# Half sums of the second weights made earlier, and the last unit's block sums dealt otherwise, in a two-level Strassen-Winograd feed-forward stage

## The chip, the cores and the metric

The kernel runs on one core of one Trainium2 chip. The metric is device time in microseconds (us) of one execution. A core has five engines that run side by side, each in its own order: PE (TensorE, matrix products into the PSUM memory), DVE (VectorE), ACT (ScalarE), POOL (GpSimd) and SP (SyncE, which here only issues DMA transfers). They wait for one another through semaphores. In the profile PE stands for matrix products and PEld for the loading of the stationary operand, which runs beside them.

## The reference

Talking-heads attention (8 batches, 12 heads, 448 positions, 64 wide) makes x of 8 x 448 x 768. A Fourier mix and a feed-forward block follow; the change lies in the feed-forward block alone.

```python
X = np.fft.fft(x, axis=1)
X = np.fft.fft(X, axis=2)
mixed = np.real(X).astype(np.float32)
u = x + mixed
mu = np.mean(u, axis=-1, keepdims=True)
var = np.mean((u - mu) ** 2, axis=-1, keepdims=True)
un = (u - mu) / np.sqrt(var + 1e-06)
ch = np.maximum(un @ w_ch1, 0.0) @ w_ch2
return (u + ch).astype(np.float32)
```

`w_ch1` is 768 x 3072 and `w_ch2` 3072 x 768. Both arrive as 64-bit floats and are turned into 32-bit ones on the chip.

## The kernel before

**Tiling.** After the attention and the mix, the feed-forward block handles the 3584 rows in 7 blocks of 512 rows (index t) and the 3072 inner columns in 6 chunks (index c). One pass over a row block and a chunk is a *unit*, n = 7c + t, so there are 42 units. Each product of a unit is a Strassen-Winograd product of 2 x 2 blocks: seven block products instead of eight, with sums before and after. The blocks are `h11`, `h12` and so on of the activations h (after the ReLU), and blocks (r, d) of the result: r is the half of the rows, d the half of the columns.

**A unit.** `first(n, ...)` makes h from the normalized input `ub` and the weights `w1t`: seven products in the order `ORDER`, six pairs of matmuls each, so 42 places that are counted in `done`. Between them DVE and ACT bring the results out of PSUM into h (copies, sums, ReLU). In chunk 0, `second` multiplies h by the second weights directly. From chunk 1 on (`DEEP = 1`) `second2` does this at two levels: each of its seven products (in the order `ORDER2`) is again seven products of quarter blocks. For the inner level, `quarters` makes sums of the quarters of h (tile `hq`, four operations, on DVE or POOL), and `halves` makes sums of the quarters of the second weights (tile `wt`, and one in place in `w2t`; four operations of 128 x 192 each).

**Half sums.** The second weights change once a chunk, so `halves` runs only in the first unit of each deep chunk (t = 0): seven sets, called set 0 to set 6 below after their place in `ORDER2`. The code calls set k ahead of product k of `first`, on DVE when k is even and on POOL when k is odd (lines 1194 and 1195).

**Order of work.** In the deep part the order of PE, DVE, ACT and POOL is that of the program text; each of these engines works strictly in order. `second2` has a list `at` of what is to be done at which of its 64 steps; seven steps belong to one outer product j (b = 7j), and the inner products stand at steps b+0, b+3, b+4, b+5, b+8, b+13 and b+16. An inner product is called by `mm`; its result is copied from PSUM into a tile `od` by `take` (ACT, L1351) or added there by `more` (DVE, L1345). Inner products of one outer product share a PSUM tile, so the next inner product that adds to this tile waits until the last result was read: the matmul of step b+16 (`psP<-wt,h`) waits for `more` of step b+11. Steps 49 and later are woven into the next unit's `first` (table `SEAM` at its first ten places); step 0 is woven in two places before the end of its own `first`.

**Ahead of that step.** Near the end of `first` DVE does: L1226 (h22 plus the fifth product, which ACT then rectifies), two pieces of background work, L1231 (h21 plus the sixth product), L1251 and L1252 (sums hs1 and hs2), four operations of `quarters` for hs2, L1255 (h21 again), then `more` of step 11. POOL does `quarters` of h11 and h22 after the fifth product, and of h12 after the seventh. In seam units the calls of `halves` stand between these.

**Background work.** `wts.deal` gives out the conversion of the next chunk's weights in small pieces (DVE L256 to L308, POOL L252, ACT L263, DMAs by SP), so many per product as the table `DEALS` says. `load_w2` fetches the next chunk's second weights, one DMA for each outer product at step b+17 of the last unit of a chunk.

**Sums of the outer level.** `both` adds one `od` tile to another (128 x 768, L1354). `out_` sends an `od` tile to the output with an adding DMA, issued by POOL (L1357): it reads the block, adds and writes it back. Two adding DMAs to one block wait for each other. The last unit (`end`) does otherwise: at step 0 it loads the blocks 11, 12 and 22 of the output into tiles `v11`, `v12`, `v22`, adds to them in memory, and stores them with plain DMAs, one half of each by SP and one by ACT (`store`, L1361). Only block 21 goes out with an adding DMA. The results of its last outer product are added to `v12` directly. Two of the last unit's block sums are on POOL.

Of the kernel before, what the change touches and what calls it, by code (L numbers as in the profile page):

```python
# [1033 lines left out]
ORDER2 = (0, 3, 5, 6, 4, 1, 2)  # L1034
UB = {(0, 0): 0, (0, 1): 6, (1, 0): 1, (1, 1): 2}
TOTALS = ((4, 6, 0), (5, 2, 4), (6, 2, 6), (3, 1, 5))
DEEP = 1
DEALS = ((2, 2, 2, 2, 2, 0, 0), (3, 4, 4, 4, 3, 0, 0))
DEST = {0: (0, 0), 1: (0, 0), 4: (1, 1), 5: (0, 1), 2: (0, 1), 6: (1, 1), 3: (1, 0)}
ACC = {0: "P", 5: "P", 6: "P", 3: "P", 1: "Q", 4: "R", 2: "R"}  # L1040
# [3 lines left out]
def ffn_phase(ctx, tc, rest, ident, u_scr, u_rev, wts, ub_scr, out, fold_rest,  # L1044
# [4 lines left out]
    nc = tc.nc  # L1049
# [28 lines left out]
    def ps_tile(key):  # L1078

        n = taken[key] = taken[key] + 1  # L1080
        more = len(pps) > 3 and key != "Q" and n % 3 == 0
        return pps[3 if more else "QPR".index(key)].tile(
            [P, 512], F32, name="ps" + key, tag="ps" + key, bufs=1 if more else 2)

    def next_part():
        if parts:
            parts.pop(0)(lambda: ppx.tile([P, 512], F32, name="ms", tag="ms"))
# [25 lines left out]
    def new_ub(n, i):  # L1113
        ubs[n, i] = lead.ub_tile(pub)
# [4 lines left out]
    def stats(t, x):  # L1119
        if x == 0:  # L1120
            mvs[t] = pst.tile([P, NT2, 3], F32, name="mv", tag="mv", bufs=2)
        st = pst.tile([P, 2, 6], F32, name="st", tag="st")
        for y in range(2):
            nc.vector.bn_stats(st[:, y, :], us[t][x][:, y * DH:(y + 1) * DH])
        nc.vector.bn_aggr(mvs[t][:, x, 0:2], st[:, :, :])

    def power(t):
        lead.power(mvs[t])
# [31 lines left out]
    def quarters(eng, hq, h, f0, f1):  # L1160

        o = hq[:, f0:f1, :, :]
        a11, a12, a21, a22 = (h[:, f0:f1, f, x * P:(x + 1) * P]
                              for x in range(2) for f in range(2))
        for to, a, b, op in ((o[:, :, 0], a21, a22, ALU.add),
                             (o[:, :, 1], o[:, :, 0], a11, ALU.subtract),
                             (o[:, :, 2], a11, a21, ALU.subtract),
                             (o[:, :, 3], a12, o[:, :, 1], ALU.subtract)):
            eng.tensor_tensor(to, a, b, op=op)  # L1169

    def halves(i, eng):

        wt[i] = right["wt"].tile([P, 3, DQ], F32, name="wt", tag=f"wt{i}")
        b11, b12 = w2[i][:, 0, :DQ], w2[i][:, 0, DQ:]
        b21, b22 = w2[i][:, 1, :DQ], w2[i][:, 1, DQ:]
        t1, t2, t4 = (wt[i][:, x, :] for x in range(3))
        for to, a, b in ((t1, b12, b11), (t2, b22, t1), (b12, b22, b12), (t4, b21, t2)):
            eng.tensor_tensor(to, a, b, op=ALU.subtract)

    def first(n, st, beside):  # L1180

        c, t = divmod(n, NTB)
        deep = c >= DEEP
        seed = n >= NTB + 2
        h = st["h"] = ph.tile([P, 7, FM, HT], F32, name="h", tag="h")
        if deep:
            hq = st["hq"] = right["hq"].tile([P, 7, 4, P], F32, name="hq", tag="hq")
        h11, h22, h21, hs1, hs2, h12, h12s = (h[:, x] for x in range(7))
        norms = c == 0 and t + 1 < NTB
        vec = nc.vector  # L1190
        ps = {}
        done = 0
        for k, i in enumerate(ORDER):
            if deep and t == 0:
                halves(ORDER2[k], (nc.vector, nc.gpsimd)[k % 2])
            if i in OPENS and ACC[i] not in ps:
                ps[ACC[i]] = ps_tile(ACC[i])
            p = ps[ACC[i]].rearrange("p (m t) -> p m t", m=FM)
            ub = ubs.pop((n, i))
            for m in range(FM):  # L1200
                for kc in range(NK):
                    for fn in beside.pop(done, ()):
                        fn()
                    done += 1
                    mm = nc.tensor.matmul(p[:, m, :], w1[i][:, kc, m * P:(m + 1) * P],  # L1205
                                          ub[:, kc, :],
                                          start=i in (0, 4, 1)[:3 - seed] and m == kc == 0,
                                          stop=kc == NK - 1, skip_group_check=True)
                    if n == k == m == kc == 0:
                        tc.keep_in_program_order(mm)  # L1210
            if i == 0 and seed:
                ps["Q"] = ps_tile("Q")
                nc.scalar.copy(out=ps["Q"][:, :], in_=ps["P"][:, :])
            elif i == 0:
                nc.scalar.copy(out=h11, in_=p)
            elif i == 4:
                nc.scalar.copy(out=h22, in_=p)
            elif i == 5:
                nc.scalar.copy(out=h21, in_=p)  # L1219
            elif i == 1 and seed:  # L1220
                nc.scalar.activation(h11, p, ACTF.Relu)
            elif i == 1:
                vec.tensor_tensor(h11, h11, p, op=ALU.add)
                nc.scalar.activation(h11, h11, ACTF.Relu)
            elif i == 6:
                vec.tensor_tensor(h22, h22, p, op=ALU.add)  # L1226
                nc.scalar.activation(h22, h22, ACTF.Relu)  # L1227
                if deep:
                    quarters(nc.gpsimd, hq, h, H11, H22 + 1)
            elif i == 2:  # L1230
                vec.tensor_tensor(h21, h21, p, op=ALU.add)  # L1231
                nc.scalar.activation(h21, h21, ACTF.Relu)
            else:
                nc.scalar.activation(h12, p, ACTF.Relu)
            x = k - 2 * (n == 0)
            if norms and 0 <= x < NT2:
                stats(t + 1, x)
                if x == NT2 - 1:
                    power(t + 1)
            if (n == 0 and k < 2) or (n == 1 and k not in (1, 2)):  # L1240
                next_part()
                if n == 0 and k == 1:
                    fold_rest(8)
            if n == 0 and k == 5:
                fold_rest()
            if deep:
                wts.deal(DEALS[t > 0][k])
            elif i != 2:
                wts.deal(2 if norms else 3)
            if i == 2:  # L1250
                vec.tensor_tensor(hs1, h21, h22, op=ALU.add)  # L1251
                vec.tensor_tensor(hs2, hs1, h11, op=ALU.subtract)  # L1252
                if deep:
                    quarters(vec, hq, h, HS2, HS2 + 1)
                vec.tensor_tensor(h21, h11, h21, op=ALU.subtract)  # L1255
            if t == NTB - 1 and c + 1 < NC:
                load_w1(c + 1, i)
            if NTB <= n + 1 < NC * NTB:
                new_ub(n + 1, i)
                nc.sync.dma_start(out=ubs[n + 1, i][:, :, :],  # L1260
                                  in_=ub_scr[(n + 1) % NTB][i])
        if deep:
            quarters(nc.gpsimd, hq, h, H12, H12 + 1)
            wts.deal(0)
        else:
            vec.tensor_tensor(h12s, h12, hs2, op=ALU.subtract)
        assert not beside
# [34 lines left out]
    def second2(n, st):  # L1302
# [5 lines left out]
        vec = nc.vector  # L1308

        def on(s, fn, *a):  # L1310
            at.setdefault(s, []).append(lambda: fn(*a))
# [65 lines left out]
            if t == NTB - 1 and c + 1 < NC:  # L1377
                on(b + 17, load_w2, c + 1, i)
        j0, j3, j5, j6, j4, j1, j2 = range(7)
        v11, v12, v22 = range(7, 10)  # L1380
        pl = nc.gpsimd
        on(12, lambda: quarters(vec, st["hq"], st["h"], H21, H21 + 1))
        on(19, lambda: quarters(vec, st["hq"], st["h"], HS1, HS1 + 1))
# [1 line left out]
                                         st["h"][:, HS2], op=ALU.subtract))  # L1385
        on(20, lambda: quarters(pl, st["hq"], st["h"], H12S, H12S + 1))
        if end:
            for v, r, d in ((v11, 0, 0), (v12, 0, 1), (v22, 1, 1)):
                on(0, load, v, r, d)
            for s, *o in ((24, vec, v11, j0), (33, vec, j5, j0), (34, pl, v12, j5),  # L1390
                          (40, vec, j6, j5), (41, vec, j3, j6), (41, pl, v22, j6),
                          (47, vec, v22, j4), (48, vec, v12, j4), (54, vec, v11, j1)):
                on(s, both, *o)
            on(42, out_, j3, 1, 0)
            on(48, store, v22, 1, 1)
            on(55, store, v11, 0, 0)
            on(61, store, v12, 0, 1)
        else:
            for s, *o in ((33, j5, j0), (40, j6, j5), (47, j5, j4), (54, j0, j1),
                          (61, j5, j2), (62, j4, j6)):  # L1400
                on(s, both, vec, *o)
            on(27, out_, j3, 1, 0)
            on(44, out_, j6, 1, 0)
            on(55, out_, j0, 0, 0)
            on(62, out_, j5, 0, 1)
            on(63, out_, j4, 1, 1)
# [46 lines left out]
    with tc.manual_schedule(engines={ET.PE, ET.DVE, ET.Activation, ET.Pool}):  # L1453
        rest_ = {}
        for n in range(DEEP * NTB, NC * NTB):
            while parts_ and sum(o[1] for o in wts.ops) < 36:
# [82 lines left out]
```

## Time and profile before

| what | us |
|---|---|
| three runs | 2323.86, 2320.95, 2319.33 |
| their median | 2320.95 |
| the profiled execution | 2327.42 |
| its span | 2325.5 |

| engine | busy us | share of the span | instructions |
|---|---|---|---|
| PE | 2258.0 | 97% | 22894 |
| PEld | 1744.6 | 75% | 22894 |
| DVE | 1715.7 | 74% | 3629 |
| ACT | 1170.0 | 50% | 3336 |
| POOL | 1278.7 | 55% | 1783 |

A deep unit takes 34.2 us (PE's rows of the same product recur at this distance, 1316.96 to 1351.16 for example). The five units with half sums begin near 1110, 1347, 1589, 1832 and 2073 us; they are called *seams* here. The span is what lies between the first and the last instruction; the time of a run has some 2 us more. In the timeline, a row merges equal neighbouring instructions (x2, x12); its columns are start, duration, engine, line, operation, operands, and in brackets the idle time of the engine just before it with the instruction that ended it. A releaser is inferred: of several things waited for, the last one is named.

### The profile page before, as it was taken

The numbers are of one execution on the slowest core, as the hardware profiler recorded it, in microseconds if no ns is written. First come the engines' busy times: TensorE is split into PE (matmuls) and PEld (weight loads), VectorE is DVE, ScalarE is ACT, GpSimd is POOL, SyncE is SP. The second block draws the span as 40 slices with busy tenths as digits, with TensorE's granted clock in tenths as the row PEclk, the third lists the DMA queues.
The fourth block names the chain that finished last, engine by engine and source line by source line (L and its number), as shares of the span: only waits on it lengthen the run. The fifth ranks groups of instructions, "written<-read, shape, count | busy, mean of one in ns | idle before, by whom it ended". The sixth has DMA issues, their size and how long they took to land.

```text
span 2325.5 us, 60782 instructions
## 1 busy us (share of the span) xinstructions
PE 2258.0 (97%) x22894; PEld 1744.6 (75%) x22894; DVE 1715.7 (74%) x3629; ACT 1170.0 (50%) x3336; POOL 1278.7 (55%) x1783
## 2 busy tenths in 40 slices
PE   6999999999999999999999999999999999999998
PEld 2455555555555667676899999999999899999997
DVE  3778878888878747777777787878778777756545
ACT  4776767666676522221355445444445445434434
POOL 3587868878777532221555454555555545444333
PEclk9999999999999999999999999999999999999999
DMA  7575665656656366667777887878877977795663
GB/s 162 163 187 165 185 179 164 191 167 189 187 161 197 135 237 197 201 207 284 215 174 192 229 220 189 221 180 243 210 174 193 283 174 179 192 257 109 148 146 68
DMA packets 231920, 439.04 MB, mean 189 GB/s; under 512 B 39624, under 2 KB 154080, under 8 KB 231630
## 3 DMA queue, kind: packets, MB, share of 16 engines
q1 hardware_dynamic: 158318, 303.56, 38.2%
q0 software_dynamic: 67312, 129.64, 30.0%
q8 instruction: 183, 3.00, 0.6%
q10 hardware_dynamic: 6000, 1.97, 0.5%
q14 instruction: 107, 0.88, 0.1%
HBM read 213.16 MB, written 142.76 MB: 153 GB/s over the span
## 4 chain that ended last, share of the span: by engine, by line
PE 84%; DVE 4%; POOL 3%; DMA 3%; ACT 2%; issue 1%; SPq 1%; ACTq 0%; DVEq 0%; POOLq 0%
PE psP L1205 17%; PE psP L1323 13%; PE psR L1205 9%; PE psR L1323 6%; PE mx L652 6%; PE ms L716 5%; PE ms L624 5%; PE psQ L1205 4%; PE po L686 4%; PE psQ L1323 3%; PE psP L1282 3%; PE ms L841 2%; DMA Kr<-Sb 2%; PE psR L1282 2%; PE ms L598 1%
## 5 line engine op out<-in xcount | busy, mean ns | idle before, releaser
L1357 POOL DMA_DIRECT2D out_dram<-od x171 | 207.8, 1277 | 260.3 <-DVE od L1345 189.4
L676 POOL TENSOR_SCALAR PP<-PP,rcp 128x448 f32<-128x448 f32 x368 | 235.7, 650 | 195.2 <-DVE rcp L674 160.6
L666 ACT ACTIVATE PP<-mx,nmx 128x448 f32<-128x448 f32 x368 | 230.2, 631 | 168.6 <-DVE nmx L659 155.1
L659 DVE TENSOR_REDUCE nmx<-mx 128x1 f32<-128x448 f32 x368 | 212.6, 618 | 95.3 <-PE mx L652 92.0
L1169 POOL TENSOR_TENSOR hq<-h 128x128 f32<-128x128 f32 (+1 forms) x210 | 127.8, 609 | 262.7 <-ACT h L1227 127.4
L1351 ACT COPY od<-psP 128x192 f32<-128x192 f32 x488 | 156.1, 320 | 181.8 <-PE psP L1323 177.2
L1354 DVE TENSOR_TENSOR od<-od 128x768 f32<-128x768 f32 x211 | 201.8, 970 | 53.8 <-ACT od L1351 52.8
L487 ACT COPY Sb<-ms 124x448 f32<-124x448 f32 (+1 forms) x384 | 184.6, 540 | 55.8 <-PE ms L624 31.1
L624 PE MATMUL ms<-kT,qT 64*32 64x448 f32 (+1 forms) x3072 | 200.1, 548 | 12.8 <-ACT qT L487 6.3
L699 DVE STREAM_TRANSPOSE Pv<-po 128x896 f32<-128x896 f32 x184 | 203.7, 1107 | 6.1 <-PE po L686 5.7
L652 PE MATMUL mx<-Kr,kw 60*32 60x448 f32 x2944 | 194.7, 550 | 8.5 <-ACT PP L666 4.7
L716 PEld LDWEIGHTS ms<-Pv,vv 64*64 64x64 f32 x5376 | 138.1, 132 | 71.6 <-issue 48.1
L686 PE MATMUL po<-PP,kw 60*32 60x448 f32 x2944 | 187.3, 539 | 3.1 <-issue 1.9
L1205 PE MATMUL psP<-qs,w1t 128*128 128x256 f32 x744 | 179.1, 380 | 0.7 <-ACT h L1219 0.7
L1205 PE MATMUL psP<-ks,w1t 128*128 128x256 f32 x744 | 179.2, 380 | 0.1
L716 PE MATMUL ms<-Pv,vv 64*64 64x120 f32 (+1 forms) x5376 | 160.9, 263 | 1.5 <-ACT X L487 0.8
L252 POOL TENSOR_SCALAR wst<-wst 128x256 f32<-128x256 f32 (+1 forms) x76 | 119.2, 1576 | 68.4 <-ACT wst L263 67.0
L1205 PEld LDWEIGHTS psP<-qs,w1t 128*128 128x128 f32 x744 | 139.6, 190 | 17.3 <-ACT h L1219 1.1
L1205 PEld LDWEIGHTS psP<-ks,w1t 128*128 128x128 f32 x744 | 139.6, 190 | 16.5 <-DVE u L1287 0.7
L1323 PE MATMUL psP<-wt,h 128*128 128x192 f32 x490 | 120.5, 328 | 12.0 <-DVE od L1345 12.0
L1205 PE MATMUL psP<-ub,w1t 128*128 128x256 f32 x528 | 127.1, 379 | 0.0
L1226 DVE TENSOR_TENSOR h<-h,psP 128x512 f32<-128x512 f32 x42 | 28.8, 687 | 130.2 <-PE psP L1205 116.6
(190 smaller groups left out, 5303.5 us busy)
## 6 DMA issues: line engine op xcount, KB each, us to landing
Kr<-Sb SPq DMA_DIRECT2D x736, 105.0 KB
out_dram<-od POOLq DMA_DIRECT2D x171, 384.0 KB, 6.9
qs<-ub SPq DMA_DIRECT2D x89, 384.0 KB
ks<-ub SPq DMA_DIRECT2D x88, 384.0 KB
ub<-ub SPq DMA_DIRECT2D x79, 384.0 KB
w1t<-w SPq DMA_DIRECT2D x42, 384.0 KB
w2t<-w SPq DMA_DIRECT2D x42, 384.0 KB
raw<-in_moe_w_ch_dram SPq DMA_DIRECT2D x32, 384.0 KB
```

Of the source, the lines that this page charges most:

```text
L624: nc.tensor.matmul(pss[x][o:o + hi - lo, :S], st["qT", xx][64 * x:64 * x + 64, y, lo:hi], st["kT", xx][64 * x:64 * x + 64, y, :], start=Tr ...
L652: nc.tensor.matmul(mx[x][64 * z + o:64 * z + o + 32, :S], kw1[64 * x:64 * x + KR, o:o + 32], Kr[64 * x:64 * x + KR, z, :], start=True, sto ...
L659: nc.vector.tensor_reduce(nmx[:, :], steps[T]["mx"][x][:, :S], axis=AX.X, op=ALU.max, negate=True)
L666: nc.scalar.activation(steps[T]["PP"][:, x, :], steps[T]["mx"][x][:, :S], ACTF.Exp, bias=steps[T]["nmx", x][:, :], accum_out=steps[T]["den ...
L676: nc.gpsimd.tensor_scalar(PP[:, x, :], PP[:, x, :], rcp[:, x:x + 1], 1.0, op0=ALU.mult, op1=ALU.mult)
L686: nc.tensor.matmul(po[o:o + 32, z, :S], kw2[64 * z:64 * z + KR, y, :], PP[64 * z:64 * z + KR, :, c * HS:(c + 1) * HS], start=True, stop=True)
L699: nc.vector.transpose(turned[a]["Pv"][:, j, :].rearrange("p (z s) -> p z s", z=2), steps[T]["po"][:, :, :S])
L716: nc.tensor.matmul(pss[y][64 * x:64 * x + 64, :nu * R], st["v", pr][64 * y:64 * y + 64, x, jb * D:(jb + 1) * D], _ap(Pv, 64 * y * rp + 32 ...
L1205: mm = nc.tensor.matmul(p[:, m, :], w1[i][:, kc, m * P:(m + 1) * P], ub[:, kc, :], start=i in (0, 4, 1)[:3 - seed] and m == kc == 0, stop= ...
L1323: nc.tensor.matmul(ps[j, key][:, :DQ], a, b, start=m in (0, 4), stop=True, skip_group_check=True)
L1354: eng.tensor_tensor(D[j][:, :, :], D[j][:, :, :], D[k][:, :, :], op=ALU.add)
L1357: nc.gpsimd.dma_start(out=acc[t, r, d], in_=D[j][:, :, :], accum_op=ALU.add)
```

## The change

A table `HALVES` says at which product of `first` which set of half sums is made, and on which engine (0 is DVE, 1 is POOL). All sets keep their engine. Set 2 goes from product 2 to 1, set 3 from 3 to 2, set 4 from 4 to 3, set 5 from 5 to 4 and set 6 from 6 to 4. So all are called at the first five products; the background pieces of `DEALS` stay with their products.

In the last unit block 22 isn't loaded, summed in memory and stored any more. The tile of j4 (with j6 added to it on DVE) goes there with an adding DMA. Block 21 gets two adding DMAs, j3 at step 27 and j6 at step 41, instead of one of their sum at step 42. The sums j3 + j6 (DVE) and v22 + j6 (POOL) are gone, v22 + j4 becomes j4 + j6, and the remaining sums and stores stand up to three steps earlier.

```diff
+HALVES = {0: ((0, 0),), 1: ((1, 1), (2, 0)), 2: ((3, 1),), 3: ((4, 0),), 4: ((5, 1), (6, 0))}
...
             if deep and t == 0:
-                halves(ORDER2[k], (nc.vector, nc.gpsimd)[k % 2])
+                for j, eng in HALVES.get(k, ()):
+                    halves(ORDER2[j], (nc.vector, nc.gpsimd)[eng])
...
-        v11, v12, v22 = range(7, 10)
+        v11, v12 = 7, 8
...
         if end:
-            for v, r, d in ((v11, 0, 0), (v12, 0, 1), (v22, 1, 1)):
+            for v, r, d in ((v11, 0, 0), (v12, 0, 1)):
                 on(0, load, v, r, d)
+            on(27, out_, j3, 1, 0)
             for s, *o in ((24, vec, v11, j0), (33, vec, j5, j0), (34, pl, v12, j5),
-                          (40, vec, j6, j5), (41, vec, j3, j6), (41, pl, v22, j6),
-                          (47, vec, v22, j4), (48, vec, v12, j4), (54, vec, v11, j1)):
+                          (40, vec, j6, j5), (45, vec, v12, j4), (46, vec, j4, j6),
+                          (52, vec, v11, j1)):
                 on(s, both, *o)
-            on(42, out_, j3, 1, 0)
-            on(48, store, v22, 1, 1)
-            on(55, store, v11, 0, 0)
+            on(41, out_, j6, 1, 0)
+            on(47, out_, j4, 1, 1)
+            on(53, store, v11, 0, 0)
             on(61, store, v12, 0, 1)
```

## The prediction, made before the changed kernel was run

> **What bounds the kernel now.** I read the page first: PE is busy 97% of the span, its clock is full in all 40 slices, and it is 84% of the chain that ended last. So only what makes PE wait counts. In part 5 one deep group has PE idle before it:
>
> ```profile
> L1323 PE MATMUL psP<-wt,h 128*128 128x192 f32 x490 | 120.5, 328 | 12.0 <-DVE od L1345 12.0
> ```
>
> The waits of PE from 1085 us to the end agree (total, times, longest; the one other entry is 0.7 us):
>
> ```profile
> PE psP L1323 <- DVE od L1345: 12.4, 7, 2.5
> ```
>
> Seven waits. PE's timeline (start, us, in brackets the idle time before) finds five of them one chunk apart, one in the first unit of each deep chunk (a "seam"), and the longest of the last two at the end:
>
> ```profile
> 1131.05 0.59 PE L1323 MATMUL psP<-wt,h 128*128 128x192 f32 x2 [2.46 <-DVE od L1345]
> 1372.57 0.59 PE L1323 MATMUL psP<-wt,h 128*128 128x192 f32 x2 [1.81 <-DVE od L1345]
> 1614.25 0.59 PE L1323 MATMUL psP<-wt,h 128*128 128x192 f32 x2 [1.98 <-DVE od L1345]
> 1857.44 0.59 PE L1323 MATMUL psP<-wt,h 128*128 128x192 f32 x2 [1.81 <-DVE od L1345]
> 2098.95 0.59 PE L1323 MATMUL psP<-wt,h 128*128 128x192 f32 x2 [1.81 <-DVE od L1345]
> 2318.89 0.59 PE L1323 MATMUL psP<-wt,h 128*128 128x192 f32 x2 [2.08 <-DVE od L1345]
> ```
>
> The five seam waits sum to 9.87 us. DVE's timeline at the second seam shows why: set 6 of the half sums stands between the last sum of h and the addition (L1345) for which PE's step 16 waits.
>
> ```profile
> 1361.66 0.69 DVE L1226 TENSOR_TENSOR h<-h,psP 128x512 f32<-128x512 f32 x1 [1.09 <-POOL wt L1178]
> ...
> 1364.15 0.69 DVE L1231 TENSOR_TENSOR h<-h,psR 128x512 f32<-128x512 f32 x1 [1.14 <-PE psR L1205]
> ...
> 1370.32 0.60 DVE L1178 TENSOR_TENSOR wt<-w2t 128x192 f32<-128x192 f32 x1
> 1370.96 0.49 DVE L1178 TENSOR_TENSOR wt<-w2t,wt 128x192 f32<-128x192 f32 x1
> 1371.38 0.60 DVE L1178 TENSOR_TENSOR w2t<-w2t 128x192 f32<-128x192 f32 x1
> 1371.90 0.34 DVE L1178 TENSOR_TENSOR wt<-w2t,wt 128x192 f32<-128x192 f32 x1
> 1372.17 0.34 DVE L1345 TENSOR_TENSOR od<-od,psP 128x192 f32<-128x192 f32 x1
> ```
>
> The set takes 1.85 us here, PE loses 1.81: without it the addition has 0.04 us to spare. The brackets are DVE's room ahead of it.
>
> **What the Trainium skill says.** "SBUF — State Buffer", section "SBUF: two separate sides": a DVE operation with two SBUF inputs and a POOL operation share one pair of ports, "an exclusive lock, not a bandwidth split". The trace agrees: a half sum takes DVE 0.35 us alone and up to 0.74 beside POOL's half sums, POOL 0.58 to 0.70. "GPSIMD Engine Reference", section "3. Performance versus the Vector engine": two-input work is about 2x slower on POOL; here 0.58 against 0.35, 1.7x. "DMA: Bandwidth & Descriptors", section "Two DMAs through the same engine are not ordered": a DMA that depends on another waits for its semaphore at the issuing engine. The trace agrees: in a usual unit j6's adding DMA, ready at 2244.5, starts at 2246.29, 6.3 us after j3's on the same block.
>
> **The seams on DVE.** The order of instructions shows the change at all five: set 6 leaves its place after L1255 and stands before L1226, set 4 goes two background pieces earlier, set 2 before the last two block sums of the unit before. No DVE instruction is added there. The removed delay is 2.64, 1.85, 2.24, 1.85 and 1.85 us, the waits are 0.04 to 0.26 less, so all 9.87 goes if L1231 starts on time; it waits for PE's sixth product, and whatever it is late becomes PE's wait.
>
> Second seam, worked through: DVE was busy from 1344 to 1360.57 but for 0.27 us, then idle 1.09 and 1.14. Set 2 moves beside POOL's two DMA issues (1349.71 to 1352.14), 1.3 us for 2.27; set 4 beside the next two (from 1356.47), 1.4 for 2.46; set 6 takes 2.46. Net +2.46 - 0.97 - 1.06 - 0.27 = +0.2: ready at 1360.8, in time. Third: set 2 gains 0.6, set 4 0.9, set 6 costs 2.5; L1226 about 0.8 late, the 1.16 idle before L1231 absorbs it. Fourth: set 6 costs 2.4, set 4 gains 0.85, idle 0.93; L1226 about 0.65 late against 1.14. Fifth: idle 3.71 and 1.81, all absorbed. PE's seventh product reads L1226's tile only 2.3 us after L1226's usual start. Were set 6 fully contended (2.65) and nothing else gained, L1231 would be late by 0.15, 1.34 and 0.58 at seams 2 to 4, 2.1 in all: the upper bound on DVE. I take none, because POOL's DMA issues leave DVE its full pace in the trace.
>
> Does set 6 wait for its load? The last of the seven w2t loads leaves SP at 1349.9; the set is due at 1358.4. In the whole deep part one half sum waited for a load (1.6 us, at 1095). SP's other moves are weight loads and stores swapped with a neighbour, a chunk ahead of their use: nothing. The two block sums behind set 2 are up to 2 us later, and the DMAs that they release stand behind POOL's set 1 anyway (1356.47).
>
> **The seams on POOL.** Here the change has a price: set 5 now stands before the quarters of h11 and h22 instead of behind them. PE's step 3 needs their first result, step 4 the second. At seam 2 POOL had 0.48 us idle there; at the first seam none:
>
> ```profile
> 1122.45 0.58 POOL L1178 TENSOR_TENSOR wt<-w2t,wt 128x192 f32<-128x192 f32 x1
> 1123.01 0.72 POOL L1169 TENSOR_TENSOR hq<-h 128x256 f32<-128x256 f32 x1
> ```
>
> Set 5 took 2.71, 3.21, 3.04, 3.20 and 3.19 us. The second quarter follows 1.45 us after POOL is free (1.8 at seam 1). Seam 2: free at 1362.6, +3.2 +1.45 = 1367.25; PE's step 4 was at 1367.19, so I put 0.2. Seam 3: 1603.8 + 3.04 + 1.45 = 1608.3 against 1608.71. Seam 4: 1851.3 against 1852.06. Seam 5: 2091.3 against 2093.58. Seam 1: 1123.0 + 2.7 + 1.8, and 0.3 because set 3 now runs beside set 6, is 1127.8 against 1124.92: PE waits 2.6 to 2.9 there, where it waited 2.46; the late DVE is hidden behind it. I put -0.3; bounds +1.0 (an uncontended POOL, sets at 2.4) and -0.9.
>
> Seams: -0.3 + 1.6 + 1.98 + 1.81 + 1.81 = 6.9 us.
>
> **The last unit.** It loses a load and two stores, a sum on DVE and one on POOL. POOL's slow sum held DVE, and ACT's part of the store of block 22 held ACT (its copy at 2317.51 had stood 3.26 us):
>
> ```profile
> 2313.48 2.58 POOL L1354 TENSOR_TENSOR od<-od 128x768 f32<-128x768 f32 x1 [0.89 <-DVE od L1354]
> ...
> 2316.10 0.96 DVE L1354 TENSOR_TENSOR od<-od 128x768 f32<-128x768 f32 x1 [0.65 <-POOL od L1354]
> ```
>
> But from 2314.25 DVE has the same list as before: three block sums and seven short additions, and the sum of v11 now stands ahead of the addition that frees PE's last matmul; before, it ran beside it. At DVE's own durations: R at 2314.25, v12 to 2315.45, two additions to 2316.0, j4 to 2316.9, two more to 2317.45, v11 to 2318.35, addition to 2318.65, PE, last addition to 2320.05, where it was 2320.24: 0.2 gained at v12's store. The other candidate is block 22's adding DMA. POOL issues j3's after its quarters, at 2309.05; j6's waits for that landing, 6.3 us later at 2315.35; j4's follows at 2316.9 and lands in 6.4 to 8.3 us (adding DMAs from 2240 on), at 2323.3 to 2325.2. The closing drains of before stood at 2324.6. So the tail is between 0.8 gained and 1.5 lost; I take 0.1 gained.
>
> **Sum.** 6.9 + 0.1 = 7.0 us. The profiled execution took 2327.42 us (span 2325.5 and 1.9 around it): 2320.4 for its like. The shown runs' median, 2320.95, is 6.5 lower; they execute the same instructions, so I carry the 7.0 over: 2314.0 us, 0.30% less. A difference of 0.2%, 4.6 us, is about what a measurement of this kernel can tell from none.
>
> **The rivals.**
> A, the forecast: seams 2 to 5 cleared, seam 1 bound by POOL: 2314.0, own range 2312 to 2316. For it: the brackets above. Chance 0.58.
> B, sharing of the ports: set 6 wholly contended (2.1 lost), and POOL's set 5 slowed as its first operation was after a DMA issue (1.65 and 2.18 us at seams 2 and 3 for 0.6 to 1.0), 1.2 at each of the first two seams: 7.0 - 2.1 - 2.4 = 2.5, so 2318.5; with DVE's part alone 2316.1. For it: half sums on both engines at once. Against: no DMA issue stands just ahead of set 5. Chance 0.24.
> C, all five cleared and 0.8 at the end: 2320.95 - 10.7 = 2310.3. Needs POOL 2.5 us faster at seam 1. Chance 0.10.
> D, slower: POOL becomes the bound. If it comes x us later to step 4 than worked out, the stalls are x at seams 1 and 2, x - 0.4, x - 0.8 and x - 2.3 at the others. At x = 2.8 these sum to 10.5 and the change loses 3.5; at 4 they sum to 16.5 and it loses 9.5: 2330. It decides from about x = 2.1, where they reach 7.0. Against: POOL's paces are measured beside a busy DVE already, and the set that it would be late by is already counted. Chance 0.08.
> That the half sums aren't moved is excluded by the order of instructions.
>
> **How the numbers follow.** Over 0.2% faster is below 2316.3: all of A but a tenth, C, and a quarter of B: 0.52 + 0.10 + 0.06, and I say 0.70 as B's lower end lies near it. Slower is D, 0.08; the rest, 0.22, is no change. The range runs from C's 2310 to just past B's 2319.5 and leaves out D and a little at either end.
>
> **What would show it.** Right: the waits of PE for L1345 fall from 12.4 us to under 3; at seams 2 to 5 step 16 has no bracket; at seam 1 PE waits at psR or psP (wt,hq) for POOL's hq, 2 to 3 us. DVE's set 2 takes about 1.3 us at seam 2, and L1231 keeps its bracket there. At the end no POOL sum stands before DVE's. Wrong: brackets for hq at seams 2 to 4, L1231 starting late without one, or the drains waiting for block 22's DMA after v12's store has landed.

## The result, and the profile after

| | us, median | lowest to highest | runs |
|---|---|---|---|
| before | 2324.84 | 2318.81 to 2336.50 | 22 |
| after | 2317.72 | 2310.47 to 2321.05 | 22 |

The ratio is 0.9964, 95% interval 0.9955 to 0.9973: 0.36% faster. The changed kernel, run once more in another comparison, gave 0.9979 (0.9968 to 0.9990). The profiled execution took 2313.94 us, its span 2312.0, 13.5 less than before.

The waits of PE from 1085 us to the end, in the trace of after (total, times, longest):

```profile
PE psP L1325 <- DVE od L1347: 2.6, 2, 1.4
PE psP L1207 <- DVE h L1228: 1.9, 2, 1.1
PE psP L1325 <- POOL hq L1170: 0.7, 2, 0.5
PE psR L1325 <- ACT h L1236: 0.7, 1, 0.7
```

All lines after the new table have moved: L1226 is now L1228, L1231 is L1233, L1345 is L1347 and so on. The row that read 12.4 us in seven waits is down to 2.6 in two. PE's timeline says where the waits of after are:

```profile
1115.66 1.99 PE L1207 MATMUL psP<-qs,w1t 128*128 128x256 f32 x8 [0.79 <-DVE h L1228]
1119.52 0.59 PE L1325 MATMUL psR<-wt,hq 128*128 128x192 f32 x2 [0.67 <-ACT h L1236]
1120.64 0.59 PE L1325 MATMUL psP<-wt,hq 128*128 128x192 f32 x2 [0.54 <-POOL hq L1170]
1600.25 0.59 PE L1325 MATMUL psP<-wt,hq 128*128 128x192 f32 x2 [0.17 <-POOL hq L1170]
1837.94 1.99 PE L1207 MATMUL psP<-ub,w1t 128*128 128x256 f32 x8 [1.14 <-DVE h L1228]
2301.76 0.56 PE L1325 MATMUL psP<-w2t,hq 128*128 128x192 f32 x2 [1.21 <-DVE od L1347]
2304.39 1.01 PE L1325 MATMUL psP<-wt,h 128*128 128x192 f32 x2 [1.42 <-DVE od L1347]
```

The first three are at seam 1, then one each at seams 3 and 4, and two in the last unit; no step 16 at a seam has a bracket. (The 0.67 is POOL's too: its first quarter ended at 1119.46, 0.06 before the matmul; ACT's L1236 is merely the last releaser on record.) DVE's timeline at seam 2, to be held against the rows at 1361.66 to 1372.17 of before:

```profile
1354.76 0.68 DVE L1228 TENSOR_TENSOR h<-h,psP 128x512 f32<-128x512 f32 x1
...
1357.08 0.69 DVE L1233 TENSOR_TENSOR h<-h,psR 128x512 f32<-128x512 f32 x1 [0.60 <-PE psR L1207]
...
1362.52 0.94 DVE L1257 TENSOR_TENSOR h<-h 128x512 f32<-128x512 f32 x1
1363.38 0.34 DVE L1347 TENSOR_TENSOR od<-od,psP 128x192 f32<-128x192 f32 x1
```

The four rows of set 6 are gone from ahead of L1347, and 0.60 us of idle is left ahead of L1233 where there had been 1.09 and 1.14.

**Stage by stage.** In the deep part PE executes the same instructions in the same order in all kernels here, so a stage can be timed from one of its instructions to the same one in another trace. The trace also says what clock PE was granted: there are stretches of 3.4 or 6.8 us at half speed, not at the same places in every execution (before: at 642, 837 and 1615 us among others; after: at 34 and 41), and one at the very end. Half of each is taken out, but for the one at the end. Us gained against before:

| | seam 1 | 2 | 3 | 4 | 5 | seams | units between | last unit, to the span's end |
|---|---|---|---|---|---|---|---|---|
| predicted | -0.3 | 1.6 | 1.98 | 1.81 | 1.81 | 6.9 | 0 | 0.1 |
| after | 1.02 | 1.72 | 1.69 | 0.36 | 2.08 | 6.87 | 0.0 | -1.15 |
| after, again | 0.59 | 1.70 | 1.70 | 1.06 | 2.08 | 7.13 | 0.0 | -1.53 |

So the stages give the change 5.7 us here. Of the other 7.7 of the profile's 13.5, 5.1 are the half-clock stretches at 642 and 837 us and 0.9 is a difference in the first 1100 us; both lie ahead of all that was changed and are not its doing. That part took 1101.8 to 1110.3 us, half clock taken out, in 14 profiles of 13 kernels: single executions differ by more than the change is worth, so below the stages decide, and times only where their intervals allow. Stages scatter too: in the five traces with the changed places of all sets (these two and three below) the seams gained 5.94 to 7.17 us in all. Seams 2, 3 and 5 agree within 0.1 us; seam 1 ranged from 0.09 to 1.02 and seam 4 from 0.36 to 1.13.

The last 1.7 of the 7.7 are the stretch at 1615 us, and that one may belong to the change. It began 0.5 us after PE's wait of 1.98 at seam 3 was over. Only two other traces have such a stretch in the deep part ahead of its end, the run with the old places and the one with set 2 on POOL (both below), each within 0.9 us of the end of a wait of 2.46 or 3.39 us; the eleven traces in which PE waited at most 2.07 us at the seams have none. (Not every longer wait has one.) The means over all runs point the same way. From the granted clock of each run one can estimate the time lost, (1 - clock) times the span: 13.2 us for the changed kernel in its second comparison against 14.8 before, and 16.8 against 14.1 with set 2 on POOL. So fewer waits of PE may also mean less half clock, and medians may show more than the stages: the first interval, some 6 to 10.5 us, lies above 5.7. No run tests this.

### The profile page after: what moved, and what is told of

Read it like the earlier page. It is cut to its first block, busy times and chain, and to the rows that moved or that the text cites. A ratio compares the mean times of both kernels' runs of the same rounds, so it can differ in the third digit from the quotient of the medians.

```text
span 2312.0 us, 60775 instructions
## 1 busy us (share of the span) xinstructions
PE 2251.5 (97%) x22894; PEld 1738.0 (75%) x22894; DVE 1719.8 (74%) x3628; ACT 1170.2 (51%) x3336; POOL 1277.2 (55%) x1784
## 4 chain that ended last, share of the span: by engine, by line
PE 83%; POOL 4%; DVE 4%; DMA 3%; ACT 2%; issue 1%; SPq 1%; ACTq 0%; DVEq 0%; POOLq 0%
PE psP L1207 17%; PE psP L1325 13%; PE psR L1207 9%; PE psR L1325 7%; PE mx L652 6%; PE ms L716 5%; PE ms L624 5%; PE po L686 4%; PE psQ L1207 4%; PE psQ L1325 3%; PE psP L1284 3%; PE ms L841 2%; PE psR L1284 1%; DMA Kr<-Sb 1%; PE ms L598 1%
## 5 line engine op out<-in xcount | busy, mean ns | idle before, releaser
L1228 DVE TENSOR_TENSOR h<-h,psP 128x512 f32<-128x512 f32 x42 | 28.8, 686 | 127.6 <-PE psP L1207 104.9
L1325 PE MATMUL psP<-w2t,hq 128*128 128x192 f32 x490 | 122.4, 332 | 1.2 <-DVE od L1347 1.2
```

What stands on the lines that cost most here:

```text
L1325: nc.tensor.matmul(ps[j, key][:, :DQ], a, b, start=m in (0, 4), stop=True, skip_group_check=True)
```

## The experiments

The theory: the half sums' places carry the gain, by what stands ahead of PE's step 16; the last unit carries none. Rivals: the last unit carries it; the early places of sets 2 to 5 are what counts; POOL or the sharing of SBUF ports sets what is left. (SBUF is the memory where the tiles lie that are not in PSUM.)

**Each part alone.** First the new places with the old last unit (the second and third parts of the diff undone):

> The changed places of the half sums, with the last unit as it was before the change. Theory (the five seams carry the whole gain, the last unit carries none or loses a little): 6 to 7 us less than before, a ratio of 0.9970 to 0.9975; in the trace PE's waits for L1345 fall to those of the last unit alone (2 of them, some 2.5 us), and the stretch from the last matmul to the end of the span is as before, 14.6 us less the end of PE's work counted from its last stall. Rival (the gain comes from the shorter last unit): within 0.1% of before, ratio 0.9990 to 1.0010.

Then the old places with the new last unit:

```diff
-                for j, eng in HALVES.get(k, ()):
-                    halves(ORDER2[j], (nc.vector, nc.gpsimd)[eng])
+                halves(ORDER2[k], (nc.vector, nc.gpsimd)[k % 2])
```

> The half sums where they were before the change, with the changed last unit (block 22 by an adding DMA). Theory: between no change and 1.1 us more than before, ratio 1.0000 to 1.0005, since in the trace of the changed kernel two additions into v12 and j4 stand ahead of the P additions that PE waits for; the five seams keep their waits for L1347 of some 1.5 to 2 us each. Rival (the last unit carries the gain): 3 us or more less, ratio 0.9987 or lower.

| | ratio to before, 95% interval | seams gained | last unit gained |
|---|---|---|---|
| new places, old last unit | 0.9956 (0.9943 to 0.9969) | 6.72 | 0.03 |
| old places, new last unit | 0.9997 (0.9982 to 1.0013) | 0.75 | -1.32 |

The whole gain is in the seams, and the new last unit costs 1.2 to 1.8 us in the seven traces that have it. (By its median the first run gained more than the 6 to 7 us expected; by the stages it gained 6.75.) PE's waits in the two traces agree: the run with the old places keeps five waits of 1.81 to 2.46 us for `more` at the seams, the other has none of them.

The 0.75 are all at seam 1, with the half sums where they always were. There PE waited 0.67 us in the kernel before for an ACT copy (L1219), and not at all in this run. In ACT's order the copy stands behind L263, which waits for a load of raw weights; in other runs the wait was 0.1 to 1.4 us or absent. About 0.7 us of the seams' 6.87 is therefore such luck, and some 6.1 are the half sums'.

**Set 6 alone** (edits are against the changed kernel where nothing else is said).

```diff
-HALVES = {0: ((0, 0),), 1: ((1, 1), (2, 0)), 2: ((3, 1),), 3: ((4, 0),), 4: ((5, 1), (6, 0))}
+HALVES = {0: ((0, 0),), 1: ((1, 1),), 2: ((2, 0),), 3: ((3, 1),), 4: ((4, 0), (6, 0)), 5: ((5, 1),)}
```

> Sets 0 to 5 stand where they stood before the change; only set 6 is made two products earlier, behind set 4 in the same product; last unit as changed. Theory (what counts is that set 6 no longer stands between L1228 and L1233 and ahead of the step-11 addition): at the seams PE's waits for L1347 fall from 9.9 us to about 3.8 us (1.5, 0.4, 1.3, 0.6, 0 at seams 1 to 5), the gain over before is about 5 to 6 us, ratio 0.9974 to 0.9979. Rival (the earlier places of sets 2 to 5 are what make room; set 6 alone only pushes the lateness into the h operand): a gain of less than 4 us, ratio above 0.9983, with waits of PE for L1228 or L1233 of over 1 us at three seams or more.

Ratio 0.9971 (0.9958 to 0.9984). Seams gained 1.17, 1.06, 1.31, 1.09 and 1.85: 6.48 of the 6.87. Step 16 waited 0.76 and 0.72 us at seams 2 and 4 and not at the others (at 1 and 3 the same step of the third outer product waited 0.18 and 0.19), about half of what was expected in all, and L1228 held PE 1.54 us at seam 1 alone. With the last unit's loss of 1.31 that is 5.2 us, within the 5 to 6 expected (the ratio's interval, 3.7 to 9.8 us, holds it). The rival falls: moving the one set out from ahead of `more` is nearly all of the gain. The four other moves add 0.6, 0.4 and 0.2 us at seams 2, 3 and 5 in all five traces with them, and lose up to 0.7 and 1.1 at seams 4 and 1; in sum they can't be told from nothing.

**Set 5 back.**

```diff
-HALVES = {0: ((0, 0),), 1: ((1, 1), (2, 0)), 2: ((3, 1),), 3: ((4, 0),), 4: ((5, 1), (6, 0))}
+HALVES = {0: ((0, 0),), 1: ((1, 1), (2, 0)), 2: ((3, 1),), 3: ((4, 0),), 4: ((6, 0),), 5: ((5, 1),)}
```

> The changed kernel with POOL's set 5 one product later, where it stood before the change. Theory (set 5 standing ahead of POOL's quarters is what makes PE wait for hq at seams 1 and 3): PE's waits for POOL's quarters (0.54 and 0.67 us at seam 1, 0.17 us at seam 3) go, those for L1228 at seams 1 and 4 stay within 0.3 us of 0.79 and 1.14 us; a wait for L1347 at step 16 of 0.3 to 0.9 us may come back at one or two seams, since set 5 then runs beside VectorE's chain. Time within 1.5 us of the changed kernel, ratio to before 0.9957 to 0.9972. Rival (the waits for hq come from set 3, or from the DMA issues on POOL): they stay as they are.

Ratio 0.9965 (0.9953 to 0.9977); seams gained -0.10, 1.70, 2.03, 1.52 and 1.85, 7.00 in all. The waits for POOL's quarters are gone, as the theory had it, and 0.1 to 0.3 us at step 16 came back at seams 2 and 4. Two things were not expected. L1228 held PE longer at seam 1, 1.40 us, in an execution in which an ACT copy had cost it 1.28 us just before. (That is not the reason, it seems: another run below with the same seams had 1.38 for the copy and none for L1228. What sets this wait at seam 1, 0 to 2.07 us in these traces, stays open.) And at seam 4 its wait disappeared. DVE's timeline there in the changed kernel, set 6 and what follows:

```profile
1834.55 0.75 DVE L1179 TENSOR_TENSOR wt<-w2t 128x192 f32<-128x192 f32 x1
1835.33 0.63 DVE L1179 TENSOR_TENSOR wt<-w2t,wt 128x192 f32<-128x192 f32 x1
1835.88 0.74 DVE L1179 TENSOR_TENSOR w2t<-w2t 128x192 f32<-128x192 f32 x1
1836.55 0.74 DVE L1179 TENSOR_TENSOR wt<-w2t,wt 128x192 f32<-128x192 f32 x1
1837.21 0.67 DVE L1228 TENSOR_TENSOR h<-h,psP 128x512 f32<-128x512 f32 x1
```

POOL's timeline in the same stretch: set 5, four operations from 1834.41 to 1837.07, wholly beside it. The same rows of DVE with set 5 back:

```profile
1842.26 0.35 DVE L1179 TENSOR_TENSOR wt<-w2t 128x192 f32<-128x192 f32 x1
1842.64 0.36 DVE L1179 TENSOR_TENSOR wt<-w2t,wt 128x192 f32<-128x192 f32 x1
1842.92 0.35 DVE L1179 TENSOR_TENSOR w2t<-w2t 128x192 f32<-128x192 f32 x1
1843.19 0.35 DVE L1179 TENSOR_TENSOR wt<-w2t,wt 128x192 f32<-128x192 f32 x1
1843.46 0.68 DVE L1228 TENSOR_TENSOR h<-h,psP 128x512 f32<-128x512 f32 x1
```

1.20 us against 2.66 for the same set, with POOL idle from 1842.40 on. That is the contention of the prediction's rival B, at one seam; it isn't the same each time (in the repeat of the changed kernel the set took 2.0 us there and PE's wait was 0.28).

**Set 2 on POOL too**, to see how near POOL is to being the bound:

```diff
-HALVES = {0: ((0, 0),), 1: ((1, 1), (2, 0)), 2: ((3, 1),), 3: ((4, 0),), 4: ((5, 1), (6, 0))}
+HALVES = {0: ((0, 0),), 1: ((1, 1), (2, 1)), 2: ((3, 1),), 3: ((4, 0),), 4: ((5, 1), (6, 0))}
```

> The changed kernel with set 2 on POOL too: POOL makes four sets at a seam, three of them ahead of its quarters and set 5 as before, VectorE three. Theory (POOL has 0 to 0.8 us to spare at seams 1 to 4, 2.3 at seam 5, and takes some 2.7 us for a set): PE waits for hq or for what hangs on it 2 to 3 us more at each of seams 1 to 4 and under 1 us at seam 5, 8 to 11 us in all, so that the gain is gone: ratio to before 0.9985 to 1.0020. Rival (POOL's DMA issues and idle stretches hide the set, and a lighter VectorE pays): waits for hq of under 1 us a seam, ratio to before below 0.9970.

Ratio 1.0030 (1.0017 to 1.0044). PE's waits from 1085 us on:

```profile
PE psR L1325 <- POOL hq L1170: 8.6, 4, 3.4
PE psP L1325 <- DVE od L1347: 2.6, 2, 1.4
PE psP L1325 <- POOL hq L1170: 1.6, 4, 0.7
PE psP L1207 <- DVE h L1228: 0.8, 1, 0.8
```

10.2 us for POOL's quarters: 4.13, 2.59, 1.92 and 1.56 at seams 1 to 4, none at seam 5. The gain of the seams is gone (-0.96), and the kernel is slower than before, by somewhat more than was expected. POOL had next to nothing to spare at the first four seams: one set more ahead of its quarters is rival D.

**Fewer background pieces at the seams.** On top of set 5 back:

```diff
-DEALS = ((2, 2, 2, 2, 2, 0, 0), (3, 4, 4, 4, 3, 0, 0))
+DEALS = ((1, 1, 1, 1, 0, 0, 0), (3, 4, 4, 4, 4, 0, 0))
```

> The kernel with set 5 back at product 5, and in the first unit of each deep chunk four background pieces for the weights of the next chunk where ten stood (one after each of the first four products), the six others dealt one each to the fifth product of the six other units. Theory (L1228 is late at seams 1 and 4 because background pieces stand ahead of it on VectorE): PE's wait for L1228 at seam 1 falls from 1.40 us to 0.3 us or less, the step-16 waits of 0.18 and 0.29 us go, no new wait in the other units; the five seams lose under 0.5 us together, and the kernel is 0.5 to 1.7 us below the one with set 5 back, ratio to before 0.9955 to 0.9965. Rival (L1228 is late by the half sums' own contention with POOL): the wait at seam 1 stays above 1 us.

Ratio 0.9990 (0.9977 to 1.0003), against the expectation. The seams did what the theory said: no wait of PE at any of the five, 10.97 us gained. But the units between lost 4.05, where the table of the stages has 0.0, and the last unit 1.53. DVE's timeline in the fourth unit of the first deep chunk:

```profile
1225.21 0.69 DVE L1228 TENSOR_TENSOR h<-h,psP 128x512 f32<-128x512 f32 x1 [2.72 <-PE psP L1207]
1225.82 0.55 DVE L295 TENSOR_TENSOR wst<-wst,tmp 128x384 f32<-128x384 f32 x1
1226.29 0.35 DVE L256 TENSOR_SCALAR wst<-wst 128x384 uint32<-128x384 uint32 x1
1226.68 1.11 DVE L283 SCALAR_TENSOR_TENSOR wst<-raw,wst 128x384 uint32<-128x384 uint32 x1
1227.82 0.77 DVE L287 TENSOR_SCALAR tmp<-wst 128x384 uint32<-128x384 uint32 x1
1228.51 0.68 DVE L1233 TENSOR_TENSOR h<-h,psR 128x512 f32<-128x512 f32 x1
```

The piece added to the fifth product is the fourth between L1228 and L1233, and L1233 has no bracket: it is late, and so is step 16 (by 0.2 to 0.6 us in two or three units of each of the first four deep chunks, mostly too short for a bracket at PE; in the last chunk, which has no next one to prepare, nothing is lost). Ahead of L1228 DVE is idle for 2.72 us. So the piece was in the wrong product, and the last experiment of this row moves it:

```diff
-DEALS = ((2, 2, 2, 2, 2, 0, 0), (3, 4, 4, 4, 3, 0, 0))
+DEALS = ((1, 1, 1, 1, 0, 0, 0), (4, 4, 4, 4, 3, 0, 0))
```

with the old last unit.

> Set 5 at product 5, four background pieces at a seam as in the run with light deals, but the six others dealt to the first product of the other units (four there where three stood) and not to the fifth; last unit as before the change. Theory (in the run with light deals the extra piece of the fifth product stood between L1228 and L1233 and made step 16 of units 3 to 5 late, 3.6 us in all; VectorE is idle for 1.7 us ahead of L1228 in a usual unit, so a piece in the first product costs nothing): no PE wait at any seam and none at step 16 of the other units, the stretch from 1110 us to the last unit 9.5 to 10.7 us shorter than before the change, last unit as before; 2.5 to 4 us below the changed kernel run beside it. Rival (any sixteenth piece ahead of L1233 makes these units late): a loss of 2 us or more in units 3 to 5 of the deep chunks, and a time within 1.5 us of the changed kernel.

Beside it ran the same kernel with the pieces as they were, and the changed kernel once more:

> The half sums of the run with set 5 back, the background pieces of the changed kernel, the last unit as before the change. Theory (parts add): the five seams gain 7.0 us over before, as in the run with set 5 back, and the last unit neither gains nor loses, so 0.8 to 1.3 us less than the changed kernel in the trace aligned on PE. Rival (parts do not add): the deep part gains less than 6 us or the last unit is more than 0.5 us longer than before's.

> The changed kernel once more, on the same chip as the two runs beside it and with the same runs of the kernel before: ratio 0.9955 to 0.9973 again if its time is that of the first comparison; in the trace the same seven waits of PE (0.8 and 1.1 us for L1228, some 1.4 us in all for POOL's quarters, 2.6 us in the last unit).

| | ratio to before, 95% interval | seams | units between | last unit |
|---|---|---|---|---|
| pieces in the first product | 0.9953 (0.9935 to 0.9971), 8 runs | 10.68 | 0.0 | 0.24 |
| pieces as they were | 0.9964 (0.9952 to 0.9976) | 7.79 | 0.0 | 0.23 |
| the changed kernel again | 0.9979 (0.9968 to 0.9990) | 7.13 | 0.0 | -1.53 |

PE's waits from 1085 us on, in the first of the three:

```profile
PE psP L1325 <- DVE od L1347: 2.8, 3, 2.1
```

Two of these (0.41 and 2.09) are in the old last unit; one, 0.30, is at step 16 of seam 1, where none was expected. The deep part is 10.7 us shorter than before the change, the most of what was expected, and the version is 5.3 us below the changed kernel beside it in the trace (10.9 against 5.6) and 5.2 in the medians (2318.88 against 2324.07), more than the 2.5 to 4 expected, though the intervals just overlap. By the stages it gains the most of all kernels here. The parts add: the middle row gains 7.8 and 0.2, where 7.0 and 0 were expected.

**The last unit.** In the changed kernel two block sums, v12+=j4 and v11+=j1, stand ahead of additions for which PE waits. DVE's timeline of after, at its end:

```profile
2300.12 0.96 DVE L1356 TENSOR_TENSOR od<-od 128x768 f32<-128x768 f32 x1
2301.00 0.61 DVE L1347 TENSOR_TENSOR od<-od,psP 128x192 f32<-128x192 f32 x2
...
2303.11 0.96 DVE L1356 TENSOR_TENSOR od<-od 128x768 f32<-128x768 f32 x1
2303.99 0.35 DVE L1347 TENSOR_TENSOR od<-od,psP 128x192 f32<-128x192 f32 x1
```

The experiment puts the sums behind them:

```diff
-                          (40, vec, j6, j5), (45, vec, v12, j4), (46, vec, j4, j6),
-                          (52, vec, v11, j1)):
+                          (40, vec, j6, j5), (46, vec, v12, j4), (47, vec, j4, j6),
+                          (54, vec, v11, j1)):
...
-            on(47, out_, j4, 1, 1)
-            on(53, store, v11, 0, 0)
+            on(48, out_, j4, 1, 1)
+            on(55, store, v11, 0, 0)
```

> The changed kernel with three block sums of the last unit moved behind the addition that PE waits for: v12+=j4 from step 45 to 46, j4+=j6 from 46 to 47 (its DMA to 48), v11+=j1 from 52 to 54 (its stores to 55). Theory (these sums stood ahead of the P additions): PE's two last waits, 1.21 and 1.42 us, fall to under 0.3 us each, the last matmul is 2 to 2.6 us earlier against the fifth seam, and the span ends 1 to 2.5 us earlier. Rival (the end is set by the stores and the adding DMA, not by PE): the waits go, and the end of the span does not move by more than 0.4 us.

Ratio 0.9977 (0.9966 to 0.9988). One of the two waits went, the other stayed at 1.54 (two sums now stand ahead of step 53's addition); PE ended 0.9 us earlier in the last unit than in after. The span's end did not move: -1.17 against -1.15. The rival is right: PE no longer sets the end. Next, which transfer does; from this kernel the adding DMA of j6 is left out, so block 21 lacks j6's part:

```diff
-            on(41, out_, j6, 1, 0)
```

> The run with late sums, with the adding DMA of j6 into block (1,0) left out: that block lacks j6's part, the output is not the reference's there. Theory (the end of the span is set by the two adding DMAs on POOL's queue, which in the run with late sums moved their packets back to back for 6.9 us, the first of them after the landing of j3's): the end of the span comes 1.5 to 4 us earlier counted from PE's place in the last unit. Rival (v12's stores and their landing set it): it moves by less than 0.5 us.

-1.32: it did not move either, so the theory of two DMAs in a row falls. A third form of the last unit, on the seams of the run with pieces in the first product, has one adding DMA less than the changed kernel, and v12's and v11's sums behind the additions:

```diff
-            for v, r, d in ((v11, 0, 0), (v12, 0, 1), (v22, 1, 1)):
+            for v, r, d in ((v11, 0, 0), (v12, 0, 1)):
...
-                          (40, vec, j6, j5), (41, vec, j3, j6), (41, pl, v22, j6),
-                          (47, vec, v22, j4), (48, vec, v12, j4), (54, vec, v11, j1)):
+                          (40, vec, j6, j5), (41, vec, j3, j6), (47, vec, j4, j6),
+                          (54, vec, v12, j4), (54, vec, v11, j1)):
...
-            on(48, store, v22, 1, 1)
+            on(48, out_, j4, 1, 1)
```

> The run with the extra piece in the first product, with a third form of the last unit: j3+=j6 on VectorE and one adding DMA for block (1,0), j4+=j6 and one for block 22, v12+=j4 and v11+=j1 both behind the P addition of step 53, no store and no load of block 22. Theory (PE's last waits come from sums ahead of the P additions, the end from the DMAs): PE's two last waits fall from 0.41 and 2.09 us to under 0.8 us together, PE ends 1.5 to 2.3 us earlier in the last unit than before the change, and the span ends within 1 us of before's last unit, since two adding DMAs still go back to back from about the same moment. Rival (the adding DMA that waits for j3's landing was all that was late): the span ends 1.5 us or more earlier than with before's last unit, and the time is 1.5 us below the run with the extra piece in the first product.

In this kernel v12 takes j4 after j6 was added to it, so block 12 gets a sum that doesn't belong there; the work is of the same kind and size. Ratio 0.9953 (0.9940 to 0.9966), the seams' gain included. PE's waits were 0.41 and 0.36, it ended 1.7 us earlier in the last unit than before the change, and the span's end came at -0.25: as the theory had it.

In all 14 traces it is 8.9 to 9.6 us from POOL's issue of the last adding DMA to the end of the span, whatever form the last unit has; from the last sum of v11 it is 5.5 to 8.6, from DVE's last addition 4.9 to 7.4. POOL's timeline, before, after and with the late sums:

```profile
2316.02 1.19 POOL L1357 DMA_DIRECT2D out_dram<-od  x1
```

```profile
2300.19 1.20 POOL L1359 DMA_DIRECT2D out_dram<-od  x1 [2.26 <-DVE od L1347]
2303.03 1.20 POOL L1359 DMA_DIRECT2D out_dram<-od  x1 [1.64 <-DVE od L1347]
```

```profile
2308.37 1.20 POOL L1359 DMA_DIRECT2D out_dram<-od  x1 [2.17 <-DVE od L1347]
2311.41 1.20 POOL L1359 DMA_DIRECT2D out_dram<-od  x1 [1.84 <-DVE od L1347]
```

The spans end at 2325.5, 2312.0 and 2320.3: 9.5, 9.0 and 8.9 us after the last of these rows. The last one is block 22's since the change; it stands behind j4+=j6, and counted from the same PE instruction its issue is 1.6 us later than that of block 21's only DMA before.

The adding DMA isn't the last to land, though: v12's two stores land after it in every trace, 0.7 to 2.0 us later. What else hangs on its issue is seen in the closing instructions. When all is issued, SP waits for the landings, and POOL's queue closes with a DRAIN that lasted until 7.7 to 8.5 us after POOL's last issue; the closing semaphores go round after both. The closing DRAINs before and after (shortest, median and longest in ns, first and last start; POOL's long one is the first):

```profile
L1534 POOLq DRAIN  x3: 46/103/9700, 2314.7 to 2325.2; - x3
L1534 SPq DRAIN  x3: 7/7/7, 2324.6 to 2324.9; - x3
```

```profile
L1537 POOLq DRAIN  x3: 46/103/8188, 2303.0 to 2311.7; - x3
L1537 SPq DRAIN  x3: 7/7/7, 2310.4 to 2311.5; - x3
```

Before, POOL's ended at 2324.37 and SP's closing ones at 2324.70: SP, held by v12's stores, was last. After, the stores landed at 2309.98 and SP was through at 2310.50, but POOL's DRAIN lasted until 2311.19. In all seven traces with the changed last unit POOL's ended later, by 0.35 to 0.69 us; in the seven others SP's did, by 0.12 to 0.69, and the span ended 0.8 to 1.1 us after the later of the two. So the end of the changed kernel is set by POOL's queue, and the loss follows from the later issue.

This also explains the two misses: late sums left the issue where it had been (0.1 us later), and so did leaving out j6's DMA. There the two ends nearly meet: v12's stores were issued 1.0 to 1.3 us earlier in the unit than in after and took 5.8 and 6.0 us to land instead of 3.9. The third form moved the issue, with other things: 1.1 us earlier than in after, and the end came 0.9 us earlier. No run moved it alone.

## Why the prediction was right, and where it was not

Forecast were 2314.0 us and 7.0 us gained (0.30%); measured were 0.36 and 0.21% in two comparisons, and 5.6 to 5.7 us by the stages. The time was 2317.72, 3.7 above the forecast, since the kernel before took 3.9 more here than in its three earlier runs. The range held, and of the cases A, the forecast, comes nearest.

- **The mechanism** (set 6 ahead of `more`, "all 9.87 goes if L1231 starts on time") is confirmed: without the last unit's part the gain stays, without the new places it goes, and set 6 alone brings 6.48 of 6.87. With the seams cleared entirely, the run with pieces in the first product gains 10.68, which is about the 9.87 and the 0.7 to 0.8 of ACT's copy at seam 1.
- **Seams 2, 3 and 5**: 1.72, 1.69 and 2.08 for 1.6, 1.98 and 1.81. At seam 2 set 2 took the predicted 1.3 us (1343.70 to 1344.98), L1233 kept a bracket; POOL's 0.2 us at step 4 didn't show. At seam 3 the quarters held PE for 0.17, where 0.4 was to spare.
- **Seam 4**, 1.81 predicted, 0.36 and 1.06 measured: the failed term is "set 6 costs 2.4, set 4 gains 0.85", L1226 "about 0.65 late against 1.14". Sets 2 and 4 took 2.5 and 2.6 us there, where they had taken 1.7 and 2.6 before, since POOL's sets and not its DMA issues ran beside them; set 4 gained nothing, and set 2 lost 0.8. The sentence "POOL's DMA issues leave DVE its full pace" was right about the issues and wrong about what would stand beside the sets: on both engines the moved sets meet one another. Besides, the allowance was measured at the wrong operation. PE's seventh product adds to the PSUM tile that L1228 has to have read, and was late by 1.14 us before L1233's room came into play; the prediction named that product's 2.3 us and then reckoned with L1231.
- **Seam 1**, -0.3 predicted, 1.02 and 0.59 measured: PE waited for POOL's quarters as said, but 1.2 us instead of 2.6 to 2.9 (set 5 took 2.4 there, not 3.0), and 0.79 for L1228, which the prediction had hidden behind POOL; with set 5 back the first wait went. Some 0.7 us of the gain is ACT's copy, which the forecast did not count.
- **The last unit**, 0.1 predicted, -1.15 to -1.53 measured: the bounds were +0.8 and -1.5, and the value that I took of them was wrong. The step that failed is the choice of v12's store as what ends last. The sign of being wrong, drains that wait for block 22's DMA after that store has landed, came: the store landed at 2309.98, POOL's DRAIN behind the DMA's issue ended at 2311.19. That the DMA itself would land last, as the lower bound had it, did not come; it had landed at 2309.30. PE's last two waits (1.21 and 1.42 for 0.40 and 2.08) no longer matter.
- **The sum** was near in part by luck, because the errors offset: +1.3 at seam 1, of which 0.7 is ACT's copy, -1.45 at seam 4, -1.25 at the end, and small ones.
- **Rivals.** B's contention lengthened sets at several seams, but is shown to cost PE time at seam 4 alone. C would have needed the seams wholly cleared; that took set 5's old place and other shares of background work as well. D begins one set further on, as the run with set 2 on POOL shows.

## What to carry to other kernels

Where an engine works in order, ask of every instruction of no urgency what urgent one stands behind it; moving one such group out from ahead of the addition that the busy engine waits for was nearly the whole gain, and what the other moves add in sum can't be told from nothing. Before moving work earlier, find the gap with an idle bracket that it is to fill, and look at what the neighbour engine does in it: the same four operations took 1.2 or 2.7 us. At the end of a kernel look at which closing wait ends last and follow it back to the issue of a transfer, since making the compute engines faster there moved nothing.

## What the runs showed of the hardware

- Two-input operations of DVE and POOL in SBUF slow one another: a half sum took DVE 0.34 to 0.36 us alone and mostly 0.63 to 0.78 beside POOL's. The Trainium skill ("SBUF — State Buffer", section "SBUF: two separate sides") describes the shared pair of ports as an exclusive lock. The set 6 shown at seam 4 agrees with that: each of its operations started 0.14 to 0.18 us after one of POOL's set 5 and took 0.63 to 0.75 us, about as long as POOL's beside it (0.59 to 0.70).
- Half-clock stretches of 3.4 or 6.8 us fell at places that differ between executions (one near 840 us is in twelve of the 14 traces), and one of 6 to 10 us at each end. One cost half its length where PE was busy: with half of before's stretch at 1615 us taken out, seam 3 of the run with the old places agrees with before's to 0.04 us. The first 1100 us differed by up to 8.5 us between executions of the same instructions. Medians of 22 runs of one kernel differed by 6 us between two comparisons (the changed one: 2317.72 and 2324.07).
- An adding DMA of 384 KB landed 5.3 us after its issue, and the next one, which waits for it, was issued at 5.9 (2294.34 to 2300.19 in after). The last one landed 5.8 to 6.7 us after its issue in the 14 traces, and POOL's closing DRAIN ended at 7.7 to 8.5.
